# Threshold attention and two MoE layers: where the row maxima are transposed

## The chip, the cores and the metric

The kernel runs on one core of one Trainium2 chip. The metric is the device time of one execution in microseconds (us). A profiled execution also has a span, from its first instruction to its last, and what lies around the span is a few microseconds of start and end.

The engines are named as in the profile: PE is TensorE (PEld its weight loads), DVE is VectorE, ACT is ScalarE, POOL is GpSimd, and SP is SyncE, whose queue issues most of the DMAs. An engine's name with a q (ACTq, SPq) marks what its sequencer does, such as issuing a DMA.

## What is computed

Attention over 4 batches of 8 heads with 576 rows and 64 columns, in which only the scores within `tau` of their row's maximum count, and then two MoE layers on its output. What matters here is the attention:

```
scores = scale * np.matmul(q, k.transpose(0, 1, 3, 2))
thresh = np.max(scores, axis=-1, keepdims=True) - tau
scores = np.where(scores >= thresh, scores, -1000000000.0)
scores = scores - np.max(scores, axis=-1, keepdims=True)
attn = np.exp(scores)
attn = attn / (np.sum(attn, axis=-1, keepdims=True) + 1e-09)
return np.matmul(attn, v)
```

## The kernel before

The 32 heads are worked on in 16 pairs, and a pair takes nine **units**, one for each transposed tile of scores: four of the first head, one that both heads share, four of the second. Unit `u` is unit `u % 9` of pair `u // 9`. In a unit, PE makes a tile `zt` of transposed scores from which the row maximum is already taken off (`shifted`, L363: four matmuls), ACT takes its exponential (`expo`, L387), DVE puts zeros where the shifted score is under the threshold (`mask`, L392), ACT and POOL split the result into a rounded part and a rest (`p_split`: `phi` L400, `plo` L401), and three units later PE multiplies the values by them (`values`, L424).

So that the maximum can be taken off inside `shifted`, it has to be known beforehand and to lie along the free axis. Some units ahead, PE makes the same head's scores the other way round (`scores`, L303, five tiles `sc` a head), DVE takes each tile's maxima (`row_max`, L316), and when a head has its five, `row_shift` (L326 to L330, ACT and then POOL) makes the ten columns `mr` of them. `shift_turn` (L335) transposes `mr` on PE into a PSUM tile `tm`, and `shift_store` (L340) copies that on ACT into `mt` (L343) and issues on ACT's own queue the DMA that puts it into two rows of `q_m` (L344), which `shifted` reads as part of its operand.

All these PSUM tiles, `tr` (the transposed inputs, L260), `sc`, `zt` and `tm`, come from one pool `ps_r` of three buffers of two banks each. A tile can be written when the last reader of the buffer's earlier tile is done: for `zt` the mask, for `sc` the maximum, for `tr` the split on DVE (`lo`, L269), for `tm` the copy `mt`. The values are summed in a pool `ps_av` of one buffer, which the copy `xs` (L436, `store_head`) frees for the next head.

The order is written out by hand. `ORDER` (L68) has a string for each of the nine units, and each engine gets its instructions in the order of the letters: E is `shifted` and `expo`, S a tile of scores, x its maximum, v a piece of `values`, M the mask, p `p_split`, L the end of a head (`store_head`), P what is in `pe_` (`transpose_kq` and `shift_turn`), A what is in `act_` (`row_shift`, `shift_store`), T the stacking and loading, J a step of decoding the weights. A head's maxima are turned `TURN_AT` = 3 units after its last tile of scores:

```
at(pe_, t + TURN_AT, shift_turn, 2 * p + j)
at(act_, t + TURN_AT, shift_store, 2 * p + j)
```

That is at P and A of unit 6 for the first head of the pair to come, and at P and A of unit 1 for the second head of the pair at work. The two places are called here **the first turn** and **the second turn**. Behind the first one stands `zt` of unit 7, behind the second one `zt` of unit 2. Both of these units have an L, so `xs` follows soon on ACT, and unit 2 has a `transpose_kq` at P and a `stack_q` at T: the DMA `q_st<-lo` (L291), the last part of an operand for the scores of unit 4, which the SP queue issues behind the two DMAs of `store_head`.

Of the kernel before, what the change touches and what calls it, by code (L numbers as in the profile page):

```python
# [9 lines left out]
F32 = mybir.dt.float32  # L10
# [11 lines left out]
def kernel(  # L22
# [15 lines left out]
    nc = tc.nc  # L38
    P = 128
# [8 lines left out]
    HS = S // 2  # L48
    NTI = 5
# [11 lines left out]
    U0 = -18  # L61
    T_A, T_B = -16, -10
    S_UNITS = (-10, -9, -7, -7, -6, -5, -4, -3, -3, -2)
    TURN_AT = 3
    JOB_EVERY = 14


# [35 lines left out]
    def f32(ap):  # L103
        return ap.bitcast(F32)
# [11 lines left out]
    ps_r = scores_ps.enter_context(tc.tile_pool(name="ps_r", bufs=3, space=PSUM))  # L116

    x = const.tile([P, KD, NT], F32, name="x")
    ident = const.tile([P, P], F32, name="ident")
# [27 lines left out]
    def buf(h):  # L147
        return h % 2, (h // 2) % NBUF[h % 2]
# [183 lines left out]

    mr_t = {}

    def shift_turn(h):  # L335
        ps = ps_r.tile([P, 1024], F32, tag="r", name="tm")
        nc.tensor.transpose(ps[0 : 2 * NTI, 0:P], f32(mr_t.pop(h)).rearrange("p l n -> p (l n)"), ident)
        mr_t[h] = ps

    def shift_store(h):  # L340
        j, i = buf(h)
        mt = att_p.tile([2 * NTI, P], F32R, tag="mt", name="mt", bufs=2)
        nc.scalar.copy(mt, mr_t.pop(h)[0 : 2 * NTI, 0:P])  # L343
        nc.scalar.dma_start(f32(q_m[j][i][R1:R3, :]), f32(mt))  # L344


# [10 lines left out]
        return (2 * p + 1,), n - 5  # L357

    st_ps = {}
    e_t = {}  # L360
    ph_t = {}

    def shifted(u):  # L363
        heads, n = unit(u)
        ps = ps_r.tile([P, 2, 512], F32, tag="r", name="zt")
        todo = []
        for h in heads:
            j, i = buf(h)
            if n is None:
                cols = slice(4 * P, SP) if j == 0 else slice(0, P)  # L370
            else:
                cols = slice(P * (j + n), P * (j + n) + P)
            todo += [(k_st[j][i][:, cols], q_st[j][i]), (k_on[j][i][:, cols], q_m[j][i])]
        for m, (st, mv) in enumerate(todo):
            for c in range(2):
                nc.tensor.matmul(  # L376
                    ps[:, c, 0:HS],
                    lhsT=st,
                    rhs=mv[:, c * HS : (c + 1) * HS],
                    start=(m == 0),  # L380
                    stop=(m == len(todo) - 1),
                )
        st_ps[u] = ps

    def expo(u):
        e = att_p.tile([P, 2, HS], F32, tag="e", name="e", bufs=4)
        nc.scalar.activation(out=e, in_=st_ps[u][:, :, 0:HS], func=ACTF.Exp)  # L387
        e_t[u] = e
# [248 lines left out]
    first_, last_, pe_, act_, late_ = {}, {}, {}, {}, {}  # L637
    by_letter = {"F": first_, "L": last_, "P": pe_, "A": act_, "T": late_}

    def at(d, u, f, *args):  # L640
        d.setdefault(max(u, U0), []).append((f, args))

    def run(d, u):
        for f, args in d.get(u, ()):
            f(*args)

    for p in range(NP):
        for j in range(2):
            h = 2 * p + j
            t = (T_FIRST, T_SECOND)[p][j] if p < 2 else UNITS * p + (T_A, T_B)[j]  # L650
# [20 lines left out]
    for p in range(NP):  # L671
        for n, d in enumerate(S_UNITS):
            at(s_at, UNITS * p + d, None, 2 * p + n // NTI, n % NTI)
        for j in range(2):
            t = UNITS * p + S_UNITS[NTI * j + NTI - 1]
            at(act_, t + 1, row_shift, 2 * p + j)
            at(pe_, t + TURN_AT, shift_turn, 2 * p + j)
            at(act_, t + TURN_AT, shift_store, 2 * p + j)
    def attention_unit(u):
        av = []  # L680
        for w, j in ((u - LAGV - 1, 1), (u - LAGV, 0), (u - LAGV, 1)):
            if 0 <= w < NU:
                heads, n = unit(w)
                if (j == 0) == (w == u - LAGV) if n is None else heads[0] % 2 == j and w == u - LAGV:
                    av.append(values(w, j))
        av = itertools.chain(*av)
        sc = iter(s_at.get(u, ()))
        mx = iter(s_at.get(u, ()))
        for what in ORDER[u % UNITS]:
            if what == "E" and 0 <= u < NU:  # L690
                shifted(u)
                expo(u)
            elif what == "v":
                next(av, None)
            elif what == "S":
                for _, a in itertools.islice(sc, 1):
                    scores(*a)
            elif what == "x":
                for _, a in itertools.islice(mx, 1):
                    row_max(*a)  # L700
            elif what == "M" and 0 <= u < NU:
                mask(u)
            elif what == "p" and 0 <= u - 1 < NU:
                p_split(u - 1)
            elif what == "V":
                for _ in av:
                    pass
            elif what in by_letter:
                run(by_letter[what], u)
            elif what == "J" and u >= JOBS_FROM:  # L710
                jobs.step("asb" if u < 0 else DECODE[u % UNITS])
# [288 lines left out]
    for n in range(len(order) + LAGO):  # L1000
# [3 lines left out]
        if n < len(order):  # L1004
# [11 lines left out]
            j = JG * g + jj  # L1016
# [97 lines left out]
```

## Time and profile before

| | us |
|---|---|
| median of three runs | 1000.67 |
| the three runs | 996.61, 1000.67, 1002.05 |
| profiled execution | 997.45 |
| its span | 995.6 |

| engine | busy us | share of the span |
|---|---|---|
| PE | 953.3 | 96% |
| PEld | 840.2 | 84% |
| DVE | 707.0 | 71% |
| POOL | 604.0 | 61% |
| ACT | 499.3 | 50% |

Busy time says how much work an engine had, not whether it was waited for. In the rows of the timeline the first number is the start, the second the time to the end of the last of the instructions that are put together (x2, x4). Matmuls overlap, so the end of one row lies behind the start of the next, and the time that PE gives away is read from the starts.

### The profile page before, as it was taken

Reading aid. Unit: us, or ns where it says so; the run is one execution under the profiler, and the core shown is the slowest. Engines: PE = TensorE matmul, PEld = TensorE weight load, DVE = VectorE, ACT = ScalarE, POOL = GpSimd, SP = SyncE. Lnnn points to the kernel's source line nnn. Section 1 sums busy time; section 2 is a strip of 40 time slices with the busy share of each in tenths; the row PEclk is TensorE's granted clock in tenths of the full one; section 3 lists DMA queues with packets and bytes.
Section 4 is the critical chain, followed back from the end, with each engine's and each line's share of the span. In section 5 each row is a group of like instructions: output and inputs, shape, how many; then the busy total and the mean of one; then the engine's idle time right before and its main releaser. Section 6 shows DMA issues by size and latency. Waiting matters only on the chain.

```text
span 995.6 us, 15113 instructions
## 1 busy us (share of the span) xinstructions
PE 953.3 (96%) x5232; PEld 840.2 (84%) x5232; DVE 707.0 (71%) x1128; ACT 499.3 (50%) x926; POOL 604.0 (61%) x573
## 2 busy tenths in 40 slices
PE   4999999999999999999999999999999999999998
PEld 3889888898898898889988998899889988888886
DVE  3678777778778765598858885887766576566661
ACT  3576776676676667444433333333334434434433
POOL 6477777887897788677535653555357804443422
PEclk9899999999999999999999999999999999999999
DMA  6555566566665421322221222122301214444443
GB/s 157 121 130 135 132 132 164 135 156 145 157 149 113 103 67 33 99 76 66 83 74 58 70 65 74 45 74 72 117 22 54 64 42 118 127 117 126 125 125 92
DMA packets 89885, 99.89 MB, mean 100 GB/s; under 512 B 50032, under 2 KB 62640, under 8 KB 89808
## 3 DMA queue, kind: packets, MB, share of 16 engines
q1 hardware_dynamic: 89424, 98.76, 38.7%
q8 instruction: 41, 0.67, 0.3%
q14 instruction: 36, 0.29, 0.1%
q10 hardware_dynamic: 384, 0.16, 0.1%
HBM read 55.13 MB, written 15.88 MB: 71 GB/s over the span
## 4 chain that ended last, share of the span: by engine, by line
PE 63%; DVE 14%; ACT 6%; POOL 6%; issue 6%; DMA 2%; SPq 2%; ACTq 1%; POOLq 0%; DVEq 0%
PE y L788 19%; PE h L750 19%; PE av L424 7%; PE zt L376 6%; PE sc L303 4%; DVE e L392 3%; POOL plo L401 2%; PE o L943 2%; PE h L832 2%; ACT e L387 2%; DVE so L860 2%; PE tr L260 2%; DVE so L887 2%; DVE st L848 1%; DVE so L872 1%
## 5 line engine op out<-in xcount | busy, mean ns | idle before, releaser
L401 POOL TENSOR_TENSOR plo<-e,phi 128x576 fp32r<-128x576 f32 x144 | 206.2, 1437 | 68.3 <-ACT phi L400 65.6
L771 POOL TENSOR_TENSOR gl<-cl,gh 128x512 fp32r<-128x512 f32 (+1 forms) x80 | 100.4, 1256 | 166.1 <-ACT gh L770 92.7
L788 PE MATMUL y<-gh,wg 128*128 128x512 f32 (+1 forms) x640 | 186.8, 373 | 0.0
L750 PE MATMUL h<-xh,wg 128*128 128x512 f32 (+1 forms) x640 | 184.1, 369 | 0.7 <-DVE e L392 0.7
L392 DVE SCALAR_TENSOR_TENSOR e<-zt,ntau,e 128x576 f32<-128x576 f32 x144 | 116.8, 812 | 78.6 <-ACT e L387 77.8
L387 ACT ACTIVATE e<-zt 128x576 f32<-128x576 f32 x144 | 93.7, 651 | 84.9 <-PE zt L376 69.2
L788 PEld LDWEIGHTS y<-gh,wg 128*128 128x128 f32 x640 | 118.8, 188 | 17.1
L750 PEld LDWEIGHTS h<-xh,wg 128*128 128x128 f32 x640 | 118.5, 188 | 17.4 <-DVE e L392 0.9
L788 PE MATMUL y<-gl,wg 128*128 128x512 f32 (+1 forms) x320 | 120.0, 375 | 0.5 <-POOL gl L771 0.4
L316 DVE TENSOR_REDUCE mcol<-sc 128x1 f32<-128x576 f32 x160 | 116.7, 748 | 3.2 <-PE sc L303 2.8
L750 PE MATMUL h<-xl,wg 128*128 128x512 f32 (+1 forms) x320 | 118.0, 369 | 0.0
L767 ACT ACTIVATE cl<-cl,half 128x512 f32<-128x512 f32 (+1 forms) x80 | 54.4, 680 | 98.3 <-DVE cl L766 98.0
L943 PE MATMUL o<-wg,ln 128*128 128x512 f32 x432 | 103.0, 394 | 0.4 <-ACT ln L906 0.4
L770 ACT CAST gh<-cl 128x512 fp32r<-128x512 f32 (+1 forms) x80 | 46.3, 579 | 111.6 <-DVE cl L769 105.0
L832 PE MATMUL h<-wg,y 128*128 128x512 f32 x432 | 101.1, 390 | 0.0
L943 PEld LDWEIGHTS o<-wg,ln 128*128 128x128 f32 x432 | 80.7, 188 | 19.9 <-ACT ln L906 1.8
L400 ACT CAST phi<-e 128x576 fp32r<-128x576 f32 x144 | 96.2, 668 | 0.9 <-DVE e L392 0.9
L832 PEld LDWEIGHTS h<-wg,y 128*128 128x128 f32 x432 | 81.0, 188 | 16.8
L907 POOL TENSOR_TENSOR ln<-land,ln 128x1024 fp32r<-128x1024 f32 x16 | 38.8, 2427 | 91.7 <-ACT ln L906 91.7
L766 DVE TENSOR_SCALAR cl<-h 128x512 f32<-128x512 f32 (+1 forms) x80 | 50.6, 632 | 56.2 <-PE h L750 52.3
L376 PE MATMUL zt<-q_st,k_both 128*128 128x288 f32 x320 | 75.6, 318 | 7.0 <-ACT mt L343 5.2
L303 PE MATMUL sc<-k_both,q_st 128*128 128x288 f32 x320 | 72.2, 308 | 5.3 <-DMA q_st<-lo 3.5
(107 smaller groups left out, 1871.9 us busy)
## 6 DMA issues: line engine op xcount, KB each, us to landing
raw<-in_moe_w_in_dram SPq DMA_DIRECT2D x24, 512.0 KB
raw<-in_moe_w_out_dram SPq DMA_DIRECT2D x24, 512.0 KB
k_both<-q_st SPq DMA_DIRECT2D x30, 288.0 KB
sq<-so SPq DMA_DIRECT2D x64, 128.0 KB
land<-sq SPq DMA_DIRECT2D x16, 512.0 KB
k_both<-lo SPq DMA_DIRECT2D x32, 144.0 KB
q_st<-lo SPq DMA_DIRECT2D x32, 144.0 KB
x<-xs SPq DMA_DIRECT2D x32, 144.0 KB
```

Of the source, the lines that this page charges most:

```text
L303: nc.tensor.matmul(ps[:, c, 0:HS], lhsT=st[j][i][r, n * P : n * P + P], rhs=kk[j][i][r, o + c * HS : o + (c + 1) * HS], start=(st is q_st) ...
L316: nc.vector.tensor_reduce(mc[:, n : n + 1], sc_ps.pop((h, n))[:, :, 0:HS], axis=AXES.XY, op=ALU.max, negate=True)
L376: nc.tensor.matmul(ps[:, c, 0:HS], lhsT=st, rhs=mv[:, c * HS : (c + 1) * HS], start=(m == 0), stop=(m == len(todo) - 1),)
L387: nc.scalar.activation(out=e, in_=st_ps[u][:, :, 0:HS], func=ACTF.Exp)
L392: nc.vector.scalar_tensor_tensor(out=e, in0=st_ps.pop(u)[:, :, 0:HS], scalar=ntau[:, 0:1], in1=e, op0=ALU.is_ge, op1=ALU.mult)
L400: nc.scalar.copy(hi, e)
L401: (nc.vector if u - NU in LO_DVE or u < NU - UNITS and u % UNITS in LO_UNITS else nc.gpsimd).tensor_tensor(lo, e, f32(hi), op=ALU.subtract)
L750: nc.tensor.matmul(ps, lhsT=a[:, kk, f], rhs=m[:, kk, :], start=(n == 0 and kk == 0), stop=(n == 2 and kk == KD - 1),)
L771: nc.gpsimd.tensor_tensor(gl, cl, f32(gh), op=ALU.subtract)
L788: nc.tensor.matmul(y_ps[c][d], lhsT=a[:, jj, ds_], rhs=m, start=(jj == 0 and n == 0), stop=(jj == JG - 1 and n == 2),)
L832: nc.tensor.matmul(ps[g], lhsT=a[:, kk, :], rhs=wg_t["in2", g][s][:, kk, :], start=(n < 2), stop=(n >= 6 * KD - 2),)
L943: nc.tensor.matmul(ps, lhsT=a[:, f, :], rhs=wg_t["out2", f // 4][m][:, f % 4, :], start=(n == 0), stop=(n == len(terms) - 1))
```

## The change

The tile `tm` goes. The transposed maxima are written into free columns of a tile `zt` (a `zt` uses columns 0 to 287 of each of its two banks; the ten rows of 128 go into columns 288 to 415 of the first). For this the turn moves by a unit: `TURN_AT` is 4, and `shift_turn` stands at the end of `shifted` of that unit, behind its four matmuls, and `shift_store` right behind `expo`. The copy `mt` then reads the `zt` tile. Only the first head of all, which is turned before there is a `zt`, keeps a tile of its own and its old place. 31 of 32 turns move.

```
-    TURN_AT = 3
+    TURN_AT = 4
...
-    def shift_turn(h):
-        ps = ps_r.tile([P, 1024], F32, tag="r", name="tm")
-        nc.tensor.transpose(ps[0 : 2 * NTI, 0:P], f32(mr_t.pop(h)).rearrange("p l n -> p (l n)"), ident)
-        mr_t[h] = ps
+    def shift_turn(h, ps=None):
+
+        if ps is None:
+            ps = ps_r.tile([P, 2, 512], F32, tag="r", name="tm")
+        tm = ps[0 : 2 * NTI, 0, HS : HS + P]
+        nc.tensor.transpose(tm, f32(mr_t.pop(h)).rearrange("p l n -> p (l n)"), ident)
+        mr_t[h] = tm
...
-        nc.scalar.copy(mt, mr_t.pop(h)[0 : 2 * NTI, 0:P])
+        nc.scalar.copy(mt, mr_t.pop(h))
...
+        for h in turn_in.get(u, ()):
+            shift_turn(h, ps)
         st_ps[u] = ps
...
-            at(pe_, t + TURN_AT, shift_turn, 2 * p + j)
-            at(act_, t + TURN_AT, shift_store, 2 * p + j)
+            if t + TURN_AT < 0:
+                t += TURN_AT - 1
+                at(pe_, t, shift_turn, 2 * p + j)
+                at(act_, t, shift_store, 2 * p + j)
+            else:
+                turn_in.setdefault(t + TURN_AT, []).append(2 * p + j)
...
                 shifted(u)
                 expo(u)
+                for h in turn_in.get(u, ()):
+                    shift_store(h)
```

On PE at the first turn (in pair 4; `av` are the values, `sc` the scores for the maxima) the order before is this; the words in brackets are the engines whose semaphores the instruction waits for:

```order
L424 MATMUL av<-plo,v_hi_116 128x288
L337 MATMUL tm<-ident,mr 10x128 [waits DVE_49,Pool_49]
L376 MATMUL zt<-q_st_107,k_both_102 128x288 [waits Activation_49]
L376 MATMUL zt<-q_st_107,k_both_102 128x288
L376 MATMUL zt<-q_m_112,k_both_102 128x288 x2
L424 MATMUL av<-phi,v_hi_116 128x288 x2
```

Here `tm` waits for the mask of unit 6, in whose buffer it is put, and `zt`, which gets the same buffer next, waits for the copy of `tm` on ACT. After the change the same place reads:

```order
L430 MATMUL av<-plo,v_hi_116 128x288
L380 MATMUL zt<-q_st_107,k_both_102 128x288 [waits DVE_49]
L380 MATMUL zt<-q_st_107,k_both_102 128x288
L380 MATMUL zt<-q_m_112,k_both_102 128x288 x2
L340 MATMUL zt<-ident,mr 10x128 [waits Pool_49]
L430 MATMUL av<-phi,v_hi_116 128x288 [waits Activation_49]
```

Now `zt` itself waits for the mask of unit 6, and the transpose stands behind it.

On ACT at the second turn (pair 4; `xs` is the copy of `store_head`) the order before:

```order
L400 CAST phi<-e 128x576 [waits DVE_49]
L343 CAST mt<-tm 10x128 [waits DMAHW0_49,PE_49]
L344 DMA q_m_111<-mt 2x5x128 [waits DMAHW2_49,Activation_49]
L387 ACTIVATE e<-zt 128x576 [waits PE_49,Pool_49]
L436 COPY xs<-av 128x576 [waits DMAHW3_49,PE_49]
```

and after the change:

```order
L406 CAST phi<-e 128x576 [waits DVE_49]
L393 ACTIVATE e<-zt 128x576 [waits PE_49]
L346 CAST mt<-zt 10x128
L347 DMA q_m_111<-mt 2x5x128 [waits DMAHW2_49,Activation_49]
L442 COPY xs<-av 128x576 [waits DMAHW3_49,PE_49]
```

The exponential now stands ahead of the copy and of the DMA's issue, and both stand between it and `xs`. The copy has no wait of its own for PE: the exponential ahead of it waits for the transpose, the last matmul into the tile. The mask of such a unit, on DVE, waits for the copy `mt` and no longer only for the exponential. The first turn has the same two sequences on ACT.

## Rows read from the trace of the kernel before

**Rows 1.** Windows of attention and MoE: stretch, its us, each engine's busy us, clock, DMA.

```profile
30.00:385.00 355.00, 333.59 (x2344) 311.14 (x2343) 270.82 (x369) 247.07 (x470) 279.84 (x274) 0.99 0.56 129
385.00:995.00 610.00, 604.49 (x2818) 516.55 (x2816) 424.22 (x737) 242.73 (x440) 307.26 (x238) 1.00 0.28 81
```

**Rows 2.** Waits from 28 to 382 us: who for whom, us in total, times, longest.

```profile
PEld tr L260 <- DVE e L392: 11.7, 13, 1.0
ACT e L387 <- PE av L424: 11.3, 15, 0.8
PEld zt L376 <- ACT mt L343: 8.3, 15, 0.6
...
PE tm L337 <- POOL mr L330: 1.4, 5, 0.4
```

**Rows 3.** Timeline at a first turn: start us, us, engine, line, instruction [idle before].

```profile
158.46 0.82 DVE L392 SCALAR_TENSOR_TENSOR e<-zt,ntau,e 128x576 f32<-128x576 f32 x1 [0.34 <-ACT e L387]
...
159.42 0.27 PE L337 MATMUL tm<-ident,mr 128*10 128x128 f32 x1
159.73 0.26 ACT L343 CAST mt<-tm 10x128 fp32r<-10x128 f32 x1 [0.75 <-PE tm L337]
...
160.04 0.54 PE L376 MATMUL zt<-q_st,k_both 128*128 128x288 f32 x2 [0.34 <-ACT mt L343]
...
160.68 0.43 PE L424 MATMUL av<-phi,v_hi 128*128 128x288 f32 x2
160.94 0.65 ACT L387 ACTIVATE e<-zt 128x576 f32<-128x576 f32 x1 [0.96 <-PE zt L376]
...
161.63 0.82 DVE L392 SCALAR_TENSOR_TENSOR e<-zt,ntau,e 128x576 f32<-128x576 f32 x1 [1.02 <-ACT e L387]
...
162.55 0.48 PE L376 MATMUL zt<-q_st,k_both 128*128 128x288 f32 x2
...
163.14 0.43 PE L424 MATMUL av<-phi,v_hi 128*128 128x288 f32 x2
```

**Rows 4.** Timeline at the second turn that follows it.

```profile
168.69 0.27 PE L337 MATMUL tm<-ident,mr 128*10 128x128 f32 x1
168.72 0.51 PE L376 MATMUL zt<-q_st,k_both 128*128 128x288 f32 x2
...
169.53 0.25 ACT L343 CAST mt<-tm 10x128 fp32r<-10x128 f32 x1
...
169.81 0.62 ACTq L344 DMA_DIRECT2D q_m<-mt  x1
...
170.53 0.65 ACT L387 ACTIVATE e<-zt 128x576 f32<-128x576 f32 x1 [0.75 <-PE av L424]
...
170.95 0.43 PE L303 MATMUL sc<-k_both,q_m 65*128 65x288 f32 x2
171.08 0.63 ACT L436 COPY xs<-av 128x576 f32<-128x576 f32 x1
171.22 0.82 DVE L392 SCALAR_TENSOR_TENSOR e<-zt,ntau,e 128x576 f32<-128x576 f32 x1 [1.29 <-ACT e L387]
...
172.09 0.86 PE L260 MATMUL tr<-ident,nat 128*128 128x128 f32 x5 [0.71 <-DVE e L392]
```

**Rows 5.** Timeline of the SP queue: the same DMA's issue in two pairs.

```profile
127.31 0.55 SPq L291 DMA_DIRECT2D q_st<-lo  x1
...
172.55 0.59 SPq L291 DMA_DIRECT2D q_st<-lo  x1
```

**Rows 6.** Timeline of PE: unit 4 of those two pairs.

```profile
130.49 0.43 PE L376 MATMUL zt<-q_m,k_both 67*128 67x288 f32 x2
130.95 0.51 PE L303 MATMUL sc<-k_both,q_st 128*128 128x288 f32 x2
...
175.99 0.43 PE L303 MATMUL sc<-k_both,q_st 128*128 128x288 f32 x2
```

**Rows 7.** The tile `mt`: its DMA's issue on ACT, ns min/median/max.

```profile
L344 ACTq DMA_DIRECT2D q_m<-mt x32: 617/618/1231, 25.9 to 373.0; - x32
```

More of the change, by code (lines that the diff above doesn't have):

```diff
@@ L359 @@
     st_ps = {}
+    turn_in = {}
     e_t = {}
```

## Prediction

> **What bounds the kernel now.** I read the windows first. From 385 us on PE is busy 604.5 of 610 us, so the two MoE layers are PE's work alone, the change touches nothing there, and they start when attention lets them: a microsecond saved in attention is saved at the end. In attention PE is busy 333.6 of 355 us, and DVE, POOL and ACT have 84, 75 and 108 us to spare [rows 1]. So attention is PE's work plus the places where PE stands still, and the question is which of these places the change touches and what is late there next.
>
> The table of waits names them [rows 2]. The weight loads of `tr` wait for the mask, 11.7 us in 13 pairs, 0.9 us each; the weight loads of `zt` wait for `mt`, 8.3 us in 15 pairs, 0.55 us each. Both belong to the turns: the second is the first turn, the first is the `tr` of unit 2, behind the second turn. A third row looks like ACT waiting for PE: 15 exponentials, 0.75 us each, "released" by `av`. The timeline shows what it is. At the second turn `zt` is finished by about 169.5, yet the exponential starts at 170.53, exactly 0.10 after the issue of `mt`'s DMA ends (169.81 + 0.62 = 170.43) [rows 4]. The issue holds ACT up, the exponential is late by it, so is the mask (171.22), and `tr`, which needs that mask's buffer, starts at 172.09, 0.05 after the mask's end, while PE was through with its scores at 170.95 + 0.27 = 171.22.
>
> **The first turn, now.** The mask of unit 6 ends at 158.46 + 0.82 = 159.28; `tm` starts 0.14 later at 159.42, is copied at 159.73, and only then `zt` starts, at 160.04: 0.62 us behind `tm` [rows 3].
>
> *After.* `zt` takes `tm`'s place in the wait for the mask and starts at 159.42. Its four matmuls take 160.68 - 160.04 = 0.64, so the transpose starts at 160.06 and ends at 160.33 (0.27). The exponential waits for the transpose: with the 0.10 that it takes from PE's end to ACT's start (160.41 + 0.43 to 160.94; I use 0.10) it starts at 160.43. The next ACT instruction follows 0.55 after an exponential's start (170.53 to 171.08 [rows 4]), so `mt` runs from 160.98 to 161.24. The mask now waits for `mt`: 161.28 to 162.10. The `zt` of unit 8, which needs that buffer, came 0.10 after the mask before (161.63 + 0.82 = 162.45, 162.55 [rows 3]); it comes at 162.20. So of the 0.62 us that go, 0.35 are kept and 0.27 are turned into a new wait of `zt` for the mask. In 15 pairs: 15 x 0.35 = **5.2 us**. In five of them `tm` also waited for POOL's `mr`, 1.4 us together [rows 2]; the transpose now comes 0.64 later and finds it ready: **1.4 us**. Ends: 0 (the new wait takes all) to 15 x 0.62 = 9.3.
>
> That the mask waits for a copy of ten other columns speaks against the change. No row of before shows such a pair, since `tm` had banks of its own. The Trainium skill, *PSUM — Partial Sum Buffer*, section "PSUM bank collisions raise a hardware error", says why it has to be so: two engines may not touch the same bank and quadrant of partitions at once, readers included, whatever the addresses. Without that rule the mask would start some 0.3 earlier and both turns together would be worth up to 15 x 0.27 + 13 x 0.19 = 6.5 us more; the instruction order agrees with the rule.
>
> What hides the moved copy and DMA issue here: behind them on ACT stands `xs`, which frees the only buffer of the values. It would run 0.10 after the issue, from 161.24 + 0.02 + 0.62 + 0.10 = 161.98 to 162.62, and `av` of the next head needs it at 162.20 + 0.59 (162.55 to 163.14 [rows 3]) = 162.79. Spare 0.07 us with the 0.10 of a hand-over: it just fits, and whatever makes it longer costs the same again in each pair.
>
> **The second turn.** *After*, `zt` starts at 168.69, where `tm` stood (0.03 earlier, nothing), the transpose runs from 169.33 to 169.60, and the exponential from 169.70, since ACT is free at 169.53 where `mt` stood [rows 4]. `mt` follows at 170.25 to 170.50, the mask from 170.54 to 171.36, `tr` at 171.41: 0.68 earlier than 172.09, with 0.19 left of its wait. In the 13 pairs of the wait's row: 8.8 us.
>
> Not all of it stays. The issue now stands between the exponential and `xs`: `mt`'s end 170.50, issue to 171.14, `xs` at 171.24 against 171.08, 0.16 later. `xs` holds the SP queue, and behind its two DMAs stands `q_st<-lo`, which the scores of unit 4 need. It was issued at 172.55 and those scores ran at 175.99 without a gap [rows 5, 6]: 3.44 us for the transfer. After, it is issued at 172.71 and the scores want to run at 175.31: 2.60 us. In another pair the same DMA, issued at 127.31, was already too late: the scores ran at 130.95 instead of 130.49 + 0.27 = 130.76. There the transfer took about 3.6 us. So the price is between 0 (transfers under 2.6 us) and 0.84 (3.44 and more, which eats all 0.68 and adds the 0.16). Only in few pairs does a wait of those scores show today, so I take a quarter to a third of the pairs as slow ones and 0.3 us as the mean: 13 x (0.68 - 0.30) = **4.9 us**. Ends: -2 to 8.8.
>
> **What else moves.** `mt`'s own DMA is issued about 1.2 us later at the first turn and 0.7 at the second. It is read two units later, some 4 us behind the issue, so it stays covered. The transposes cost PE the same in either place. `phi` and `plo` of those units come up to 0.3 us later and are read three units on. The last pair has no `tr` in unit 2 and its values wait for `xs` there; it may lose 0.2 to 0.5 us, which I take off.
>
> **Sum.** 5.2 + 1.4 + 4.9 - 0.5 = 11.0 us off the profiled execution's 997.45 (span 995.6 and 1.85 around it): 986.4. The median of the runs shown lies 3.2 us above that execution, so I forecast 989.6, and say **989.5 us**. Both ends together: 9.3 + 1.4 + 8.8 = 19.5 off the median, 981; and about nothing, 1000.
>
> **Rivals.**
> 1. *Only the first turn pays.* The transfer of `q_st<-lo` is 3.4 us or more in most pairs, and the scores of unit 4 take back what `tr` gained. For: the pair with 130.95. Against: the pair with 175.99, and that the table of waits has no row for it. Then 5.2 + 1.4 remain: about 994.
> 2. *Neither pays.* `xs` misses its 0.07 us, the values of the next head wait for it and swallow the first turn, and rival 1 takes the second. For: the fit is that close, and every hand-over is an estimate from one pair. About 1000, within 2 us of now.
> 3. *Slower: the DMA's issue takes longer in its new place.* It waits for an earlier DMA's semaphore as before, and at worst it took 1.23 us instead of 0.62 [rows 7], at the start of the kernel. In its old place the exponential behind it bore that; now `xs` does, at both turns. Each 0.1 us longer costs 0.1 in 15 pairs (less the 0.07 once) and 0.1 in 13 pairs through `q_st<-lo`. At 0.61 longer: 15 x 0.54 + 13 x 0.61 = 16 us, against the gain of 11: about 1005. It decides from 0.43 us longer on. Against: the median is 0.618 and all DMAs that it waits for are old by a unit or more.
> 4. That the change doesn't do what it says is excluded: the order of the instructions shows both moves.
>
> **How the numbers follow.** Chances: the forecast 0.62, rival 1 0.18, rival 2 0.13, rival 3 0.07. A measurement of this kernel can tell about 0.5%, 5 us, from no change. The forecast and most of rival 1 are faster by more than that (0.62 + 0.13); the rest of rival 1 and nearly all of rival 2 are within it (0.05 + 0.12); rival 3 and a bit of rival 2 are slower: 0.75, 0.17, 0.08. The range goes from the upper end of both gains, 981, to 998, which leaves out rival 3 and most of rival 2.
>
> **What would show it.** In the profile after, the wait of `zt` for `mt` (8.3 us) and the 15 exponentials with the odd releaser (11.3 us) should be gone; `tr`'s wait for the mask should fall from 0.9 to about 0.2 us each; a new wait of `zt` for the mask, 0.2 to 0.3 us in each pair, should stand in unit 8, and the mask should wait for `mt` in units 2 and 7. Rival 1 shows as scores of unit 4 that wait for a DMA, rival 2 as values that wait for `xs`, rival 3 as issues longer than 0.62 us. I am wrong altogether if PE's standstills in attention (355 us less its work) don't shrink, or if they shrink and the start of MoE does not come earlier.

## The result, and the profile after

The changed kernel takes 985.3 us (median of four executions, 984.05 to 988.06) where the kernel before, run beside it, takes 1000.7: a ratio of 0.987, with an interval of 0.984 to 0.990. Its profiled execution took 985.73 us with a span of 983.9. The profiled execution of before took 997.45 with a span of 995.6, so from profile to profile 11.7 us are gone. The sum in the prediction was 11.0 off that execution, and the forecast 989.5 us with a range of 981 to 998.

The windows of the changed kernel, cut where attention now ends (stretch, its us, busy us of PE, PEld, DVE, ACT and POOL, granted clock, DMA share, GB/s):

```profile
30.00:373.00 343.00, 332.62 (x2339) 307.99 (x2338) 273.28 (x369) 242.00 (x470) 278.67 (x276) 1.00 0.57 133
373.00:983.00 610.00, 605.12 (x2829) 518.11 (x2827) 427.25 (x739) 243.91 (x443) 308.03 (x238) 1.00 0.28 82
```

MoE is what it was: 605 of 610 us busy, beside [rows 1]. The windows are cut by hand, 12 us apart. In the first one PE's work stayed at 333 us, and its standstills fell from 21.4 to 10.4 us. MoE's first matmul starts at 375.9 us and not at 386.4, so 10.5 us of the 11.7 are gone by then; the other 1.2 lie behind it.

The table of waits of the changed kernel from 28 to 375 us (who for whom, us in total, times, longest):

```profile
ACT e L393 <- PE zt L340: 20.3, 16, 1.4
DVE e L398 <- ACT mt L346: 14.0, 27, 0.7
PEld zt L380 <- DVE lo L269: 7.5, 16, 0.9
...
PEld zt L380 <- DVE e L398: 5.1, 20, 0.3
...
PEld av L430 <- POOL plo L407: 4.2, 12, 0.7
...
PE zt L380 <- DVE lo L269: 3.8, 8, 0.7
...
PEld tr L260 <- DVE e L398: 1.6, 5, 1.0
...
PE sc L303 <- DMA q_st<-lo: 0.6, 1, 0.6
```

The three big rows of [rows 2] are gone or small. No `zt` waits for `mt` any more, no exponential has the odd releaser `av`, and `tr` waits for the mask in 5 pairs, 1.6 us together, where it was 13 and 11.7. New are the exponentials that wait for the transpose (L340), the masks that wait for the copy `mt`, 0.52 us each with all that lies before it, and 0.25 us each in which the weight loads of `zt` wait for the mask: 15 of these 20 stand at unit 7, whose `zt` took `tm`'s place behind the mask, and five, 0.16 us each, at unit 8, where the prediction looked for them in every pair. One group has grown that was not in the prediction: `zt` that waits for DVE's `lo`, 7.5 us of weight loads and 3.8 of matmuls, where the kernel before has 1.3 and 0.7 (28 to 382 us). The scores wait for the DMA `q_st<-lo` once.

The timeline of the changed kernel at a first turn (start us, us, engine, line, instruction, idle before), the one that [rows 3] show of before:

```profile
155.35 0.82 DVE L398 SCALAR_TENSOR_TENSOR e<-zt,ntau,e 128x576 f32<-128x576 f32 x1 [0.35 <-ACT e L393]
...
156.22 0.53 PE L380 MATMUL zt<-q_st,k_both 128*128 128x288 f32 x2
...
156.86 0.28 PE L340 MATMUL zt<-ident,mr 128*10 128x128 f32 x1
...
157.17 0.65 ACT L393 ACTIVATE e<-zt 128x576 f32<-128x576 f32 x1 [1.30 <-PE zt L340]
...
157.72 0.24 ACT L346 CAST mt<-zt 10x128 fp32r<-10x128 f32 x1
...
157.99 0.62 ACTq L347 DMA_DIRECT2D q_m<-mt  x1
...
158.04 0.82 DVE L398 SCALAR_TENSOR_TENSOR e<-zt,ntau,e 128x576 f32<-128x576 f32 x1 [0.55 <-ACT mt L346]
...
158.72 0.64 ACT L442 COPY xs<-av 128x576 f32<-128x576 f32 x1 [0.77 <-PE sc L303]
...
158.92 0.53 PE L380 MATMUL zt<-q_st,k_both 128*128 128x288 f32 x2
```

It runs in the forecast's steps: `zt` right behind the mask's end (155.35 + 0.82 = 156.17), the transpose, the exponential, the copy, the mask 0.08 behind the copy's end (157.96), and `zt` of unit 8 0.06 behind that mask's end (158.86). From one mask's end to the other `zt` it is 158.92 - 156.17 = 2.75 us, where [rows 3] give 162.55 - 159.28 = 3.27: 0.52 less in this pair.

And the second turn that follows it:

```profile
165.31 0.43 PE L380 MATMUL zt<-q_st,k_both 128*128 128x288 f32 x2
...
166.16 0.65 ACT L393 ACTIVATE e<-zt 128x576 f32<-128x576 f32 x1
...
166.97 0.62 ACTq L347 DMA_DIRECT2D q_m<-mt  x1
167.03 0.82 DVE L398 SCALAR_TENSOR_TENSOR e<-zt,ntau,e 128x576 f32<-128x576 f32 x1 [0.48 <-ACT mt L346]
...
167.69 0.64 ACT L442 COPY xs<-av 128x576 f32<-128x576 f32 x1 [0.75 <-PE av L430]
...
168.22 0.68 ACT L406 CAST phi<-e 128x576 fp32r<-128x576 f32 x1
168.23 0.80 PE L260 MATMUL tr<-ident,nat 128*128 128x128 f32 x5
...
168.98 1.43 POOL L407 TENSOR_TENSOR plo<-e,phi 128x576 fp32r<-128x576 f32 x1 [0.86 <-ACT phi L406]
...
169.24 1.45 DVE L501 TENSOR_SCALAR raw<-dec_a 128x512 uint32<-128x512 uint32 x1
...
170.61 0.81 DVE L269 SCALAR_TENSOR_TENSOR lo<-tr,scale,q_st 128x576 fp32r<-128x576 f32 x1
...
171.47 0.53 PE L380 MATMUL zt<-q_st,k_both 128*128 128x288 f32 x2 [0.39 <-DVE lo L269]
```

From `zt` of unit 2 to `tr` it is 168.23 - 165.31 = 2.92 us, where [rows 4] give 172.09 - 168.72 = 3.37. `tr` no longer waits for the mask, which ended at 167.85; PE is bound there by its own work. Then `zt` of unit 4 waits 0.39 us for `lo`, which stood on DVE behind a step of the weight decoding, `raw<-dec_a`, of 1.45 us.

**A finer measure.** The whole time varies by several us from execution to execution, and in the two kernels that were profiled twice that arises before pair 1, as is shown below. I therefore also use the time from the first exponential of pair 1 to that of pair 15, fourteen whole pairs with fourteen first and fourteen second turns. Before, these two rows:

```profile
53.13 0.65 ACT L387 ACTIVATE e<-zt 128x576 f32<-128x576 f32 x1 [0.64 <-PE zt L376]
...
370.04 0.65 ACT L387 ACTIVATE e<-zt 128x576 f32<-128x576 f32 x1 [0.47 <-PE zt L376]
```

and after:

```profile
51.48 0.65 ACT L393 ACTIVATE e<-zt 128x576 f32<-128x576 f32 x1 [0.62 <-PE zt L380]
...
359.55 0.65 ACT L393 ACTIVATE e<-zt 128x576 f32<-128x576 f32 x1 [0.41 <-PE zt L380]
```

That is 316.91 and 308.07 us. The same starts in the trace of every kernel give this table. Its columns two to four part the mean pair at the exponentials of units 1, 4, 6 and of the next unit 0: the second turn lies between units 1 and 4, the first between unit 6 and the next unit 0.

| kernel | median us | mean us, units 1 to 4 | units 6 to 0 | the rest | pairs 1 to 14, us |
|---|---|---|---|---|---|
| before | 1000.7 | 7.80 | 8.50 | 6.34 | 316.91 |
| changed | 985.3 | 7.56 | 8.07 | 6.38 | 308.07 |
| e1 first turn only | 989.6 | 7.84 | 8.08 | 6.41 | 312.71 |
| e2 second turn only | 992.8 | 7.52 | 8.46 | 6.33 | 312.28 |
| e3 own tile | 984.7 | 7.29 | 8.23 | 6.59 | 309.46 |
| e4 issue later | 990.6 | 7.15 | 8.49 | 6.49 | 309.89 |
| e5 first in zt, issue later | 985.4 | 7.27 | 8.06 | 6.41 | 304.39 |
| e6 copy behind too | 985.3 | 7.37 | 8.09 | 6.52 | 307.69 |
| e7 two issues | 1004.8 | 7.72 | 8.84 | 6.58 | 323.96 |
| e8 before again | 1000.4 | 7.80 | 8.50 | 6.35 | 316.93 |
| e9 only the first pair | 997.1 | 7.80 | 8.53 | 6.34 | 317.34 |
| e10 all but the first pair | 989.4 | 7.58 | 8.08 | 6.34 | 307.97 |
| e11 best of both | 982.7 | 7.27 | 8.05 | 6.43 | 304.50 |
| e12 changed again | 987.0 | 7.56 | 8.08 | 6.35 | 307.82 |

The two executions of one kernel agree in the last column within 0.25 us, where their spans differ by 2.2. The kernel e9, which has the turns of pairs 1 to 14 in the old place, lies 0.43 above the kernel before. So I read differences above half a us as real.

### The profile page after: what moved, and what is told of

The parts are those of the page before. It is cut to its first block, busy times and chain, and to the rows that moved or that the text cites. A ratio compares the mean times of both kernels' runs of the same rounds, so it can differ in the third digit from the quotient of the medians.

```text
span 983.9 us, 15050 instructions
## 1 busy us (share of the span) xinstructions
PE 953.3 (97%) x5232; PEld 839.6 (85%) x5232; DVE 711.5 (72%) x1128; ACT 494.6 (50%) x926; POOL 603.0 (61%) x573
## 4 chain that ended last, share of the span: by engine, by line
PE 77%; DVE 7%; ACT 5%; issue 3%; POOL 2%; SPq 2%; DMA 2%; ACTq 1%; DVEq 0%; POOLq 0%
PE y L801 20%; PE h L763 19%; PE o L956 10%; PE h L845 10%; PE av L430 7%; PE zt L380 6%; PE sc L303 4%; DVE e L398 3%; ACT e L393 2%; DVE mcol L316 2%; ACT phi L406 1%; DVE lo L269 1%; PE tr L260 1%; ACT xs L442 1%; DVE raw L501 1%
```

## Experiments: what each turn is worth

**e1: only the first turn.**

```
-            if t + TURN_AT < 0:
+            if t + TURN_AT < 0 or j == 1:
```

> The first turn is moved into zt of unit 7 as in the changed kernel; the second turn stays where it was, with a tile of its own. Theory (the two turns pay separately: mask to zt of unit 8 0.52 us shorter in 15 pairs, 7.8 us, and tm's wait for POOL 1.4 us of which the 0.52 may hold a part): 992 us, 8 to 9 under the kernel before; the wait of tr for the mask stays at 0.9 us in 13 pairs. Rival (the second turn brings nearly all, since the new wait of zt for the mask eats the first): 998 to 1001, no difference. Rival (the turns help each other): 987 or less, nearly all of the 15 us.

Measured: 989.6 us, ratio 0.991 (0.989 to 0.994). The time is near the first theory's 992, but not by its sum: that had 0.52 us a pair, 7.3 in fourteen pairs. In pairs 1 to 14 the kernel gains 4.20 us, 0.30 a pair: 0.42 at the turn, of which 0.11 goes again in the other units. From profile to profile another 2.5 us lie ahead of pair 1, where one of the moved turns stands, and 1.3 behind pair 14, where none does. The wait of `tr` for the mask stays (10.5 us, 13 times).

**e2: only the second turn.**

```
-            if t + TURN_AT < 0:
+            if t + TURN_AT < 0 or j == 0:
```

> The second turn is moved into zt of unit 2; the first stays where it was, with a tile of its own. Theory: zt to tr is 0.46 us shorter in 13 or 14 pairs, 6 us, and nothing of it is given back at the scores of unit 4: 994 to 995 us; the wait of zt for mt at the first turn stays at 0.55 us in 15 pairs. What the prediction had: 0.68 gained and 0.30 given back, 4.9 us: 996. Rival (the transfer of q_st<-lo takes it back): 1000 to 1001, with a wait of the scores of unit 4 for a DMA.

Measured: 992.8 us, ratio 0.993 (0.991 to 0.996), a little faster than the three cases expected. In pairs 1 to 14 it gains 4.63 us, 0.33 a pair, where the theory had 6, and both turns together, 8.83, are what the changed kernel gains, 8.84: in these pairs the two add up. The scores of unit 4 wait for the DMA `q_st<-lo` in two pairs (0.9 us), so the rival is out. The price is paid in another place. The waits of this kernel:

```profile
PEld zt L380 <- DVE lo L269: 8.6, 12, 0.9
...
PE zt L380 <- DVE lo L269: 5.5, 10, 0.7
```

**e3: the new order with a tile of its own.** Everything stands where the changed kernel has it, but the transpose gets a tile `tm` as before, so that no exponential waits for it and no mask for its copy.

```
         for h in turn_in.get(u, ()):
-            shift_turn(h, ps)
+            shift_turn(h)
```

> The order of the changed kernel (the transpose behind zt, the copy and the issue behind the exponential), but the transpose gets a tile of its own again. It tells the move from the shared tile. If the shared tile costs (the exponential waits 0.27 us for the transpose and the mask 0.25 us for the copy): the new wait of zt for the mask goes and it is 3 to 6 us faster than the changed kernel, 979 to 983. If the shared tile is what pays (a tile of its own takes one of three buffers, and the next tile of scores has to wait for a mask or for the copy): 990 to 1000. If only the move counts and both costs are small: 985 to 988.

Measured: 984.7 us, ratio 0.987 (0.983 to 0.990), no different from the changed kernel (in pairs 1 to 14 it is 1.4 us longer). So it is the place of the turn that pays, and the shared tile is not needed for it. The parts differ, though: the second turn is 0.27 us a pair shorter than in the changed kernel (7.29 against 7.56), the first 0.16 longer (8.23 against 8.07) and the other units 0.21 longer. A tile of its own saves the two waits and costs a buffer: the next scores wait for the copy (2.2 us, 8 times) and the mask (3.8 us, 7 times).

**e4: one line of the kernel before moved.** Only the second turn's DMA issue goes behind the exponential of unit 2. The transpose, its tile and the copy stay.

```
-        nc.scalar.dma_start(f32(q_m[j][i][R1:R3, :]), f32(mt))
+        if j == 1 and h > 1:
+            mt_t[h] = mt
+        else:
+            nc.scalar.dma_start(f32(q_m[j][i][R1:R3, :]), f32(mt))
...
                 expo(u)
+                issue_late()
```

> The kernel before, with one line moved: at the second turn the issue of mt's DMA on ACT stands behind the exponential of unit 2 and no longer ahead of it; the copy stays. Theory (the issue, 0.62 us on ACT, held up the exponential, so the mask, so tr): the exponential starts 0.65 us earlier, tr's wait for the mask falls from 0.9 to 0.2 or 0.3 us, PE is bound there next, and 13 x 0.46 = 6 us go: 994 to 995 us, as the second turn alone. Rival (the exponential waits for PE, as the table of waits has it): no difference, 1000 to 1001. Rival (the later issue makes xs late, with it q_st<-lo): no difference or slower, 1000 to 1003, with a wait for that DMA.

Measured: 990.6 us, ratio 0.991 (0.988 to 0.994), and 7.0 us in pairs 1 to 14: more than the second turn's move brings (4.6). The waits of this kernel from 28 to 382 us:

```profile
PEld zt L386 <- DVE lo L269: 3.8, 9, 0.9
...
PEld tr L260 <- DVE e L402: 1.2, 1, 1.2
```

`tr` waits for the mask once and not in 13 pairs. That shows what the row "ACT e L387 <- PE av L424" of [rows 2] was: the exponential stood behind the issue, not behind PE. And `zt` waits for `lo` half as long as in e2.

**e5: the first turn as changed, the second as in e4.** The diff is those of e1 and e4 together.

> The first turn in zt of unit 7 as in the changed kernel; the second turn stays in its old place with a tile of its own, and only its DMA's issue stands behind the exponential of unit 2. Theory (at the second turn all that was to be gained is the issue's 0.62 us; the shared tile costs there, because the exponential waits for the transpose and the mask for the copy, DVE comes 0.5 us later to the split lo, and zt of unit 4 waits for lo): the two gains add up, 4.2 us in pairs 1 to 14 for the first turn and 7.0 for the issue, where the changed kernel has 8.8: 2.4 us faster than the changed kernel, 981 to 984, and the wait of zt for lo is 4 to 6 us and not 11. Rival (the shared tile costs nothing there): 985 to 988. Rival (a turn with its own tile in between takes buffers from the moved first turn): 988 to 991.

Measured: 985.4 us, ratio 0.987 (0.984 to 0.990). By its time the rival would have it; by its pairs the theory: 304.39 us for pairs 1 to 14, 3.7 less than the changed kernel (the sum of the two gains would give 2.4), and the wait of `zt` for `lo` is down to 3.5 us. What it gained there it lost in the first pair, which took 24.26 us and not 21.16, and the mean clock is 0.994 to 0.997 in four of its five executions. The fall of the clock behind that is taken up with e8 to e10.

**e6: the copy behind the exponential too.** As e5, but copy and issue both stand behind the exponential of unit 2, the order on ACT that the changed kernel has there, with a tile of its own.

```
+                if t < 0:
+                    at(act_, t, shift_store, 2 * p + j)
+                else:
+                    store_in.setdefault(t + 1, []).append(2 * p + j)
...
+                for h in store_in.get(u, ()):
+                    shift_store(h)
```

> As the run before it (first turn in zt, second turn's transpose in its old place with its own tile), but the copy mt too stands behind the exponential of unit 2, ahead of the issue. Theory (the exponential comes 0.1 to 0.25 us earlier, but PE is bound behind it): within 2 us of the run before it. If the exponential is still what tr and zt of unit 4 wait for: 2 to 3 us faster than that. If the tile's buffer is needed before the late copy has read it: slower by 2 us or more, with scores or tr that wait for mt.

Measured: 985.3 us, ratio 0.988 (0.985 to 0.991); 307.69 us in pairs 1 to 14, 3.3 more than e5. By its time it is within 2 us of e5; by its pairs none of the three cases holds, since no `tr` and only one tile of scores (0.4 us) waits for `mt`. The loss is spread: 0.10 us a pair at the second turn, 0.03 at the first, 0.11 in the other units. The exponential is no later than in e5, and still it is slower. The only difference is where the copy stands on ACT, and with it whether the issue has to wait for the copy: from the exponential's start to `xs` it is 1.53 us in the mean, as in the changed kernel, and 0.87 in e5. So what costs is how much ACT has to do between the exponential and `xs`.

The timeline of e11, which has e5's second turn, in the pair of the rows above, shows the better order:

```profile
163.10 0.25 ACT L346 CAST mt<-tm 10x128 fp32r<-10x128 f32 x1
...
163.38 0.65 ACT L403 ACTIVATE e<-zt 128x576 f32<-128x576 f32 x1
...
163.46 0.62 ACTq L357 DMA_DIRECT2D q_m<-mt  x1
...
164.29 0.64 ACT L452 COPY xs<-av 128x576 f32<-128x576 f32 x1 [0.26 <-PE av L440]
...
165.58 1.42 POOL L417 TENSOR_TENSOR plo<-e,phi 128x576 fp32r<-128x576 f32 x1 [0.54 <-ACT phi L416]
...
166.16 1.12 DVE L511 TENSOR_SCALAR raw<-dec_a 128x512 uint32<-128x512 uint32 x1
```

Here the issue (163.46 to 164.08) lies beneath the exponential (163.38 to 164.03), because the data that it sends is already there. (That ACT's sequencer goes on while the engine works is what the Trainium skill, *Perfetto Trace Analysis*, section "DVE / Act Engine Instruction (TENSOR_ADD, Activation, etc)", leads one to expect; these rows agree.) In the changed kernel it has to wait for the copy, which waits for the exponential: it runs alone from 166.97 to 167.59, and `xs` starts 1.53 us behind the exponential's start instead of 0.91. Behind `xs` comes `phi`, and behind `phi` POOL's `plo`, which starts 168.98 - 166.16 = 2.82 us behind the exponential and not 2.20. Two rows of e6 in the same pair show what that does on DVE:

```profile
166.75 0.42 DVE L502 TENSOR_SCALAR raw<-dec_a 128x512 uint32<-128x512 uint32 x1
166.79 1.67 POOL L408 TENSOR_TENSOR plo<-e,phi 128x576 fp32r<-128x576 f32 x1 [1.16 <-ACT phi L407]
```

The decoding step takes 0.42 us when it starts just ahead of `plo`, and then `plo` takes 1.67 instead of 1.42. When it starts just behind `plo`'s start, as in the changed kernel (169.24 behind 168.98), it takes 1.45 and ends 0.28 behind `plo`'s end. In e11 `plo` starts 0.58 ahead of the step, and the step takes 1.12 and ends 0.28 behind `plo`'s end again. Whichever of the two starts first, the other waits for it. That holds throughout: in pairs 1 to 14 of all traces 124 decoding steps of the form TENSOR_SCALAR start inside a `plo`, and each ends 0.28 to 0.34 us behind that `plo`'s end. (The Trainium skill, *SBUF — State Buffer*, section "SBUF: two separate sides", has such a rule: VectorE in some of its modes and GpSimd share a pair of ports, and the instruction that gets it first holds it to its end. The three pairs of rows agree with the order of start deciding; in which mode the step runs no row tells.) So in the changed kernel a late `plo` holds up DVE, `lo` behind it, and `zt` of unit 4. In seven of the fourteen pairs of the changed kernel it is 2.99 to 3.34 us from the exponential of unit 3 to that of unit 4, in the other seven 2.40 to 2.83. In pairs 3, 8 and 11 no decoding step stands there, and `lo` is late because ACT's copy `q_st` is: 6.6 us behind the pair's first exponential and not 6.2 to 6.35 as in e11.

So a late `xs` costs in two ways, by `plo` and by `q_st`, and e6 tells them apart. Its mask doesn't wait for a copy and starts 0.7 us behind the exponential of unit 2 and not 0.9. The step then starts just ahead of `plo` in pairs 1, 2, 4, 6, 9 and 12, and from the exponential of unit 2 to that of unit 4 these take 5.7 to 5.8 us, where the changed kernel takes 6.7 to 6.8. In pairs 3, 8 and 11, by a late `q_st`, e6 is as slow as the changed kernel, 6.2 us where e11 takes 5.6 to 5.8, and that is a part of what it loses against e5. Another part are scores that wait for a mask, 3.7 us of weight loads in six places (51 to 355 us), where e5 has one of 0.2.

**e7: two issues instead of one.**

```
-        nc.scalar.dma_start(f32(q_m[j][i][R1:R3, :]), f32(mt))
+        nc.scalar.dma_start(f32(q_m[j][i][R1:R1 + 1, :]), f32(mt[0:NTI, :]))
+        nc.scalar.dma_start(f32(q_m[j][i][R1 + 1:R3, :]), f32(mt[NTI:2 * NTI, :]))
```

> The changed kernel with mt's DMA split into two, one row of q_m each, so that ACT has two issues behind each copy, 0.62 us more at both turns ahead of xs. By the prediction's third rival (0.07 us to spare at the first turn, none at the second): 15 x 0.55 + 13 x 0.62 = 16 us slower than the changed kernel, 1001. If only the first turn is as tight as that and the DMA q_st<-lo has time at the second: 8 us, 993 to 994. If xs has more time than I gave it at both: 985 to 988.

Measured: 1004.8 us, ratio 1.0065 (1.004 to 1.009), slower than the kernel before. The issues of this kernel (ns, min/median/max, first and last start):

```profile
L347 ACTq DMA_DIRECT2D q_m<-mt x32: 699/701/1467, 26.4 to 382.2; - x32
L348 ACTq DMA_DIRECT2D q_m<-mt x32: 693/700/734, 27.9 to 382.9; - x32
```

Two of them take 0.78 us more than the one of 0.618. In pairs 1 to 14 the kernel loses 15.9 us against the changed one. The first turn loses 0.77 a pair, all of the 0.78: `xs` has nothing to spare there, and the prediction's 0.07 was right to that size. The second turn loses 0.16, and the other units 0.2. The row of it (the changed kernel has 2.6 us there, 4 times):

```profile
PEld av L431 <- ACT xs L443: 10.3, 14, 1.4
```

These values that wait for `xs` are the rival's mechanism. The price of 0.78 at the second turn is not: the rival's arithmetic, with 0.78 in both, gives 15 x 0.71 + 13 x 0.78 = 20.8 us.

## Experiments: the start of attention

**e8: the kernel before once more.**

> The kernel before once more, with a second profile. Its time should be that of the kernel before, 995 to 1002, ratio 1. It is to show whether the stretch at half clock at 32 to 39 us and the first pair of 24.5 us stand in other executions of it too: if pair 0 is again over 24 us and the later pairs make 316 to 318 us, the start differs from kernel to kernel; if pair 0 takes 21 to 22 us, the start differs from run to run.

Measured: 1000.4 us, ratio 1.002 (1.000 to 1.004). The pairs 1 to 14 take 316.93, as before to 0.02 us, and pair 0 takes 25.57 where the first profile had 24.51. Ahead of the first exponential it has 1.7 us more. So the difference between these executions is made at the start, and the half clock stands in this profile as well, for 10.2 us where the first one has 6.8. The windows of the kernel before (the last three numbers: granted clock, DMA share, GB/s):

```profile
32.00:36.00 4.00, 3.77 (x16) 2.86 (x15) 2.21 (x4) 1.50 (x5) 2.83 (x2) 0.54 0.84 204
36.00:40.00 4.00, 4.00 (x20) 3.97 (x21) 2.30 (x3) 2.43 (x4) 1.42 (x1) 0.60 0.53 103
```

and what PE did ahead of the fall:

```profile
30.76 0.27 PE L337 MATMUL tm<-ident,mr 128*10 128x128 f32 x1 [0.29 <-DVE mcol L316]
31.39 0.53 PE L376 MATMUL zt<-q_st,k_both 128*128 128x288 f32 x2 [0.36 <-DVE e L392]
...
32.12 0.67 PE L303 MATMUL sc<-k_both,q_st 128*128 128x288 f32 x2
```

That is a second turn, that of pair 0, in its old place: PE stands still for 0.29 and 0.36 us around `tm`, and at 32.3 the granted clock falls from 2.4 to 1.2 GHz, until 39.2. The prediction took no notice of it.

**e9: this one turn alone.** 30 of the 31 turns stay as before.

```
-            if t + TURN_AT < 0:
+            if t + TURN_AT < 0 or not (j == 1 and p == 0):
```

> Only one of the 31 turns is moved: the second turn of the first pair, some 31 us after the start; all others stay in their old places. Theory (in its old place that turn leaves PE standing 0.65 us more just there, and most executions of the kernel before then run at half clock for about 7 us, which costs about 3.5): mean clock 0.999 or more in at least 5 of 6 executions, 995 to 998 us, pairs 1 to 14 as before (316.9 us). Rival (the drop at the start has nothing to do with this turn): 1000 us and clocks of 0.994 to 0.996 in half of the executions.

Measured: 997.1 us (twelve executions, mean clock 0.999 or more in all), ratio 0.998 (0.9965 to 1.0002, so by itself just short of a difference), while pairs 1 to 14 take 317.3 as before. Its windows:

```profile
32.00:36.00 4.00, 3.28 (x22) 2.65 (x21) 2.90 (x5) 2.87 (x6) 2.82 (x2) 1.00 0.68 174
36.00:40.00 4.00, 4.00 (x33) 4.00 (x32) 3.11 (x5) 3.28 (x8) 2.14 (x2) 1.00 0.74 165
```

**e10: the changed kernel with this one turn back in its old place.**

```
-            if t + TURN_AT < 0:
+            if t + TURN_AT < 0 or (j == 1 and p == 0):
```

> The changed kernel with that one turn, the second of the first pair, back in its old place. Theory: half clock near the start comes back in about half of the executions, median 986 to 990 us, pairs 1 to 14 as in the changed kernel (308.1 us). Rival: 985 us and clocks of 0.999 as in the changed kernel.

Measured: 989.4 us, ratio 0.990 (0.987 to 0.992), 2.4 us above the changed kernel run beside it (e12; the two ranges overlap), with pairs 1 to 14 as in the changed kernel. The mean clock lies under 0.999 in 4 of 6 executions.

Over all kernels but e7, the mean clock was under 0.999 in 46 of the 85 executions that have that turn in its old place, and in 2 of the 40 that have it behind `zt`. e7 is not counted, since its profile has a second fall, at 385.6 us, that lowers the mean as well; all five of its executions are under 0.999. It also shows that this turn is not the only thing that can bring the fall: there the turn stands behind `zt`, and the clock falls at 30.6 us, behind a standstill of 1.23 us in which `zt` waits for the DMA `q_m<-mt`. And e1 and e6, with the turn in its old place, have standstills of 0.28 to 0.41 us around `tm` in their profiles and no fall. So the place of this turn changes the chance of a fall; it is not a switch. What it is worth in time is not settled: 2.8 us of the median in e9 and 2.4 in e10, neither clear of the noise. In the 46 executions of the kernel before that ran beside e1 to e12, the 24 with a mean clock under 0.999 have a median of 1000.2 us and the others 997.1, but 10 of these 22 took 999.5 to 1003.6 without the fall.

**e11: the best of both.** First turns in `zt`, the second turn of pair 0 in `zt`, later second turns as in e4.

```
-            if t + TURN_AT < 0:
+            if t + TURN_AT < 0 or (j == 1 and p > 0):
```

(with the edit of e4)

> First turns in zt of unit 7; the second turn of the first pair in zt of unit 2; the second turns of all later pairs in their old places with a tile of their own and the DMA's issue behind the exponential. Theory (the drop at the start is gone with the moved turn of the first pair, and the issue alone is the better mend in later pairs): pairs 1 to 14 take 304.4 us, clocks 0.999, 980 to 983 us, 3 us under the changed kernel. Rival (the start differs for another reason): 985 us.

Measured: 982.7 us (981.69 to 984.95), ratio 0.984 (0.981 to 0.986): faster than the kernel before, and 4.3 us under e12 that ran beside it. Their ranges and intervals just overlap; the 3.3 us by which it is faster in pairs 1 to 14 are clear.

**e12: the changed kernel once more.**

> The changed kernel once more: 984 to 988 us, ratio 0.987 to the kernel before, pairs 1 to 14 308.1 us, mean clock 0.999 or more in all executions if the moved turn of the first pair keeps the clock up.

Measured: 987.0 us (984.04 to 988.53), ratio 0.987 (0.985 to 0.989), clocks of 0.999 and more in all six. Its profiled execution has a span of 986.1, 2.2 more than the first one, again all ahead of pair 1: the second pair's first exponential stands at 53.92 and not at 51.48. Here the granted clock doesn't tell why. The window and PE's timeline of e12:

```profile
32.00:36.00 4.00, 4.00 (x18) 3.65 (x17) 2.86 (x4) 2.01 (x4) 0.45 (x3) 1.00 0.79 172
```

```profile
36.60 0.68 PE L303 MATMUL sc<-k_both,q_st 128*128 128x288 f32 x2
37.08 0.68 PE L303 MATMUL sc<-k_both,q_m 65*128 65x288 f32 x2
```

Two matmuls of 288 columns take 0.48 us here, and 0.27 later on, though the column reads 1.00. In every trace PE starts in these steps at 18 us. It leaves them at some point between 22 us (e1 and the kernel before) and 44 us (e3); in e12 only at 38.6. These executions have a late start and no fall of the granted clock. What decides on it was not tried and stays open.

## Why the prediction was right, and where not

**What bounds the kernel.** Right: attention's standstills shrank, and MoE, which stayed as busy as it was, came 10.5 us earlier.

**The first turn.** The sum had 14 x 0.35 + 1.4 = 6.3 us for the fourteen pairs measured, 0.45 a pair. The place itself gives 0.42, so this working comes close, although some of its hand-overs were too long (`zt` follows the mask at 0.05 us, not 0.14). The 1.4 us were too much: of the five waits one stands at a second turn, and one of the other four, 0.15 us, is no longer than what `tm` waits behind the mask in the other pairs; in the three that are left 0.7 us come on top of that. And e1 keeps only 4.2 us: 0.11 a pair goes in the units around, and nothing in the sum stood for that. The rows of e1 that are larger than before are values that wait for `plo` (2.9 us of weight loads, 8 times, against 0.7 and 2) and `zt` that waits for the mask (7.1 us, 26 times, against 1.6 and 4 in the same stretch before); 14 of these waits, 4.0 us, stand at the turn itself, at `zt` of unit 7.

**`xs` at the first turn.** 0.07 us to spare, and e7 shows that it is about nothing. The copy and the issue just fit.

**The second turn.** Its term was 13 x (0.68 - 0.30) = 4.9 us, and e2 measured 4.6. The size is right and the reason is not. The 0.68 didn't come in full, since PE itself is late for `tr` next (0.45 in the pair shown). The give-back was put at the scores of unit 4, behind `q_st<-lo`; these wait for the DMA once. The pair that spoke for it, with scores at 130.95, was misread: their weight load, at 130.92, waits 0.23 us for the mask on DVE, which ends at 130.91, and so no row shows that a transfer took 3.6 us. The give-back lies at `zt` of unit 4, which waits for `lo`. The step that failed is the sentence that `phi` and `plo` "come up to 0.3 us later and are read three units on". That looked at who reads them, and not at what stands on DVE while POOL makes `plo`.

**Where the gain at the second turn comes from.** The analysis found the right cause: the issue on ACT ahead of the exponential. Moving the issue alone (e4) brings 7.0 us, 1.5 times what the turn's move brings.

**The bank rule.** The mask waits for the copy in 27 places, as the prediction read from the order of the instructions. What it costs was put at up to 6.5 us for both turns. e3, where no bank is shared, comes out at the same time: it gains 0.27 us a pair at the second turn and loses 0.37 at the first and in the other units, where the extra tile takes a buffer. What the rule costs by itself stays open, since no kernel here has banks of its own for the tile without taking a buffer.

**The last pair.** 0.5 us were taken off. From the first exponential of pair 15 to MoE's first matmul it is 16.3 us in both kernels: no loss. From that exponential to the end it is 625.6 us before, 625.1 in e8, and 624.4 in both profiles of the changed kernel, so MoE itself is 0.7 to 1.2 us shorter; the reason stays open.

**The start.** Not in the sum at all. From profile to profile the 11.7 us are 8.84 in pairs 1 to 14, 1.65 ahead of them (53.13 to 51.48) and 1.2 behind them. The sum's 11.0 had 6.6 + 4.9 for the turns of all pairs and took 0.5 off: some 2 us too much for the first turn, and nothing for the start and the end, which made up for it. A part of the closeness is luck. The 1.65 ahead of pair 1 are themselves a sum of two things that the prediction did not have: pair 0, with its two turns moved and without the fall of the clock, takes 3.35 us less, and its first exponential comes 1.7 later. The medians lie 15.4 apart because the profiled execution of before was 3.2 us under its median, although it has the fall; the prediction took these 3.2 us as an offset that stays, and the changed kernel's profile lies 0.4 above its median.

**The rivals.** The first (only the first turn pays) falls with e2, the second with e1 and e2. The third has a true mechanism, the values that wait for `xs`, and e7 shows its price; the issue in the new place takes 0.618 us as before (median of 32), so its condition was not met.

## What to carry to other kernels

Here a DMA issue on ACT's queue cost ACT's stream its full 0.62 us where it had to wait for the copy just ahead of it (166.97 to 167.59), and nothing where an exponential whose result it doesn't need ran at the same time (163.46 to 164.08 beneath 163.38 to 164.03). So look at what stands just ahead of an issue. When something is moved out of one wait, follow the displaced engine's next few outputs to the other engines that work at the same time, not only to their readers. And when whole times vary by more than the effect, measure a stretch that repeats in the trace.

## What the runs showed of the hardware that was not expected

- A DVE step on 128x512 uint32 and POOL's `plo` (128x576) hold each other up: 0.42 us for the step if it starts first (and `plo` 1.67), 1.45 if it starts 0.26 us behind `plo`, with its end 0.28 us behind `plo`'s. The mean of `raw<-dec_a` in pairs 1 to 14 is 0.66 us before, 1.13 in the changed kernel, 0.87 in e11 and 0.44 in e6.
- Standstills of PE of 0.3 to 0.4 us around one transpose stood ahead of a fall of the granted clock to 1.2 GHz, for 6.8 or 10.2 us, in a stretch where PE had just begun its steady work. In two profiles (e1, e6) they stood there without a fall. With that transpose elsewhere the mean clock was under 0.999 in 2 of 40 executions (e7 apart), and with it in its old place in 46 of 85.
- PE's matmuls run at half their later pace from 18 us until 22 to 44 us while the column of the granted clock reads 1.00.
- Half of a DMA, five partitions instead of ten, took 0.70 us to issue on ACT, and the whole 0.618: at these two sizes the issue does not get shorter with the size.
